# One core, long convolution beside routed experts: the first products, the transform of the input by pairs of positions, and two entries of the planner

## The chip, the cores and the metric

The kernel runs on one core of a Trainium2 chip. The core has a matrix engine (PE, whose weight loads are listed apart as PEld), a vector engine (DVE), a scalar engine (ACT), a general engine (POOL) and a queue engine (SP) that issues nearly all transfers. Its matmuls write to eight banks of accumulator memory. The metric is the device time of one execution in microseconds (us), lower is better. Before the change it is 1466.44 us, the median of 3 runs (1465.94 to 1466.64).

## The reference

2048 tokens `x` of width 576 pass through two branches that a gate mixes.

```python
g = sigmoid((x * gate_w).sum(-1))
# a: a long convolution of each of 576 channels with a generated filter of 2048 taps
K = einsum("dn,dnl,dn->dl", Cc, exp(dt * A * l), dt * Bc).real
a = irfft(rfft(x padded) * rfft(K padded))[:L] + x * Dskip
# b: 32 heads, two best of 64 keys on each of two sides, two best pairs, 4096 experts
s1, s2 = (x @ w_q)[..., :128] @ k1.T, (x @ w_q)[..., 128:] @ k2.T
top_s, top_e = two best of the sums of the two best of s1 and s2
b = sum over heads and choices of softmax(top_s) * gelu(x . u[top_e]) * v[top_e]
return g * a + (1 - g) * b
```

## The kernel before

All of it is written as generators in `body`, which a planner at build time interleaves. The planner keeps a clock (`clock`), a time at which each tile is ready (`rdy`, filled from costs in `act_cost`, `dve_cost`, `dma` L199 and `mm` L206), and counts of free banks (tags `sc`, `kb`, `wb`) and SBUF slots. What it makes is a fixed order of instructions for each engine. At run time nothing is reordered: an engine that meets an instruction whose input is late waits, and all behind it waits too.

**Split words.** The large products take float32 operands as two float16 words, a high and a low one. A group of 14 matmuls with 512 columns (`triple` L850) makes one bank: four slices of 128 of the contraction with three products each (high by high, high by low, low by high), and two matmuls for the last 64 rows, where high and low words are stacked (`wrem`, and slice 8 of `xb`). There are two families of 128 groups. Groups `s` are the key scores of 128 tokens and 8 heads (weights folded from `wq` and `kT` by `w_half` L518 and `wb` matmuls into `whl`). Groups `a` are the products of 128 experts of a block (`uhl`) with 512 tokens (`xb`), stored as `go` to `g_d`. Four token blocks `tb` and eight weight blocks `c` exist of each. After them follow, for each tile of 128 tokens, the one-hot products `S` and 192 matmuls `o`.

**The start.** SP loads `kT`, token block 0 (`xs`, `xr`), then the first score weights `wq`, then the first expert block (`us`, `ur`). `x_build` L446 squares the token block, bounds its norm by `x` matmuls with a matrix of ones, scales, and makes nine slices `xb`. `w_half` squares, folds and scales `wq`. `u_build` L1214 does the same for `us`. The main loop at L1563 picks `s` or `a` groups by readiness; the first one is an `s` group.

**The transform of the input** (`u_stage1` L977) takes 32 pairs of token positions, one a step, in two alternating generators `half(0)` and `half(1)`. A step loads 64 rows twice (so that the high words stand on partitions 0 to 63 and the low words on 64 to 127), loads a table `tu`, splits (`uh`: one ACT instruction and one DVE instruction on 64 partitions), runs 2 by 2 matmuls `u` of 128 rows and 288 columns, copies out and stores to `su_d`.

**The filter.** `k_front` L717 and `k_gen` make filter taps (phases by matmuls `kP`, taps by matmuls `kb`) in 36 chunks for `k_d`, on banks of tag `kb`, which the `u` matmuls share. When the last chunk is stored, `freq` L1164 loads the taps back in four parts (`ksb`) and then two tables `tk`, runs 32 steps `k` (`k_stage1` L1027), and then 36 steps of `products` L1063 (matmuls `pr`, `pi`, complex products on POOL and DVE, matmuls `pv`). The `s` and `a` groups fill PE between them.

## Time and profile before

| | us |
|---|---|
| median of 3 runs | 1466.44 |
| the profiled execution, its own time | 1466.58 |
| span of its trace, first to last instruction | 1464.7 |
| PE busy in the span | 1431.2 |
| DVE / ACT / POOL busy | 1248.5 / 790.6 / 532.0 |
| slots of `u` matmuls, first and last start | 114.8 to 558.6 |
| slots of `k` matmuls, first and last start | 662.9 to 739.0 |

The times in a trace count from the first instruction. Matmuls overlap in the records, since each is shown with its way through the array; how often they start tells what one costs in a stream. A timeline row names start, length, engine, line, operation, output and inputs, shape and count, and in brackets the idle time before it and what ended it.

### The profile page before, as it was taken

The numbers are of one execution on the slowest core, as the hardware profiler recorded it, in microseconds if no ns is written. First come the engines' busy times: TensorE is split into PE (matmuls) and PEld (weight loads), VectorE is DVE, ScalarE is ACT, GpSimd is POOL, SyncE is SP. The second block draws the span as 40 slices with busy tenths as digits, with TensorE's granted clock in tenths as the row PEclk, the third lists the DMA queues.
The fourth block names the chain that finished last, engine by engine and source line by source line (L and its number), as shares of the span: only waits on it lengthen the run. The fifth ranks groups of instructions, "written<-read, shape, count | busy, mean of one in ns | idle before, by whom it ended". The sixth has DMA issues, their size and how long they took to land.

```text
span 1464.7 us, 36789 instructions
## 1 busy us (share of the span) xinstructions
PE 1431.2 (98%) x14025; PEld 858.4 (59%) x14028; DVE 1248.5 (85%) x4589; ACT 790.6 (54%) x1315; POOL 532.0 (36%) x511
## 2 busy tenths in 40 slices
PE   5999999999999999999999999998999999999999
PEld 2445454554544544555555444455787787788787
DVE  6989989989999699959899898579998998898860
ACT  5647767698697787434656544576424224223310
POOL 0443545556745645201246799622100110110100
PEclk8999999999999999999999999999999999999999
DMA  9235433372434534384768666677533432442400
GB/s 319 81 93 162 128 94 118 111 213 89 147 104 133 160 107 135 109 263 138 254 211 290 232 200 206 221 239 221 157 111 116 133 125 85 138 147 68 156 10 17
DMA packets 139185, 221.21 MB, mean 151 GB/s; under 512 B 11648, under 2 KB 82688, under 8 KB 132608
## 3 DMA queue, kind: packets, MB, share of 16 engines
q1 hardware_dynamic: 138912, 218.78, 46.5%
q8 instruction: 110, 1.80, 0.5%
q14 instruction: 67, 0.55, 0.1%
q10 hardware_dynamic: 96, 0.07, 0.0%
HBM read 147.51 MB, written 71.30 MB: 149 GB/s over the span
## 4 chain that ended last, share of the span: by engine, by line
PE 84%; DVE 10%; DMA 3%; ACT 1%; issue 1%; SPq 1%; POOL 1%; DVEq 0%; ACTq 0%; POOLq 0%
PE o L213 24%; PE a L213 23%; PE s L213 22%; PE S L213 4%; PE wb L213 2%; PE kb L213 2%; DVE i L133 2%; PE pr L213 2%; DVE m L133 1%; PE u L213 1%; PE y L213 1%; PE kP L213 1%; DVE e L133 1%; PE pv L213 1%; DVE uh L133 1%
## 5 line engine op out<-in xcount | busy, mean ns | idle before, releaser
L213 PE MATMUL o<-vhl,wh 128*128 128x288 f16 x3072 | 387.0, 286 | 0.0
L213 PE MATMUL s<-whl,xb 128*128 128x512 f16 x1536 | 369.5, 382 | 5.0 <-DVE whl L133 4.2
L213 PE MATMUL a<-xb,uhl 128*128 128x512 f16 x1536 | 361.1, 379 | 0.4 <-DVE ko L133 0.4
L213 PEld LDWEIGHTS <-wh 128*128 128x128 f16 x3072 | 296.0, 98 | 76.3 <-issue 3.7
L213 PEld LDWEIGHTS <-xb 128*128 128x128 f16 x1792 | 171.8, 98 | 213.1 <-issue 27.1
L213 PEld LDWEIGHTS <-uhl 128*128 128x128 f16 x1536 | 148.2, 98 | 175.7 <-issue 2.8
L133 DVE FIND_INDEX8 i<-m,s 128x8 uint32<-128x64 f32 x1024 | 206.5, 222 | 0.0
L133 ACT ACTIVATE wh<-gl,s_wg 128x1024 f16<-128x1024 f32 x64 | 68.9, 1137 | 200.3 <-DVE gl L133 200.3
L133 DVE MAX8 m<-s 128x8 f32<-128x64 f32 x1024 | 146.4, 215 | 28.1 <-PE s L213 27.8
L133 POOL TENSOR_TENSOR CS<-CS,ex 128x512 f32<-128x512 f32 x72 | 100.2, 1423 | 139.0 <-DVE ex L133 120.0
L133 POOL TENSOR_TENSOR ya<-ya,db 128x576 f32<-128x576 f32 x16 | 32.0, 2012 | 305.2 <-DMA ya<-in_au_dram 143.6
L133 ACT ACTIVATE go<-a,i_a 128x512 f32<-128x512 f32 x95 | 64.2, 686 | 82.5 <-PE a L213 54.7
L133 POOL TENSOR_TENSOR e<-aN,rt 128x512 f32<-128x512 f32 x72 | 87.5, 1234 | 50.9 <-PE kb L213 47.6
L133 DVE SCALAR_TENSOR_TENSOR wh<-gl,s_wg,wh 128x1024 f16<-128x1024 f32 x64 | 92.4, 1474 | 11.3 <-ACT wh L133 11.3
L133 DVE TENSOR_TENSOR gl<-S,gl 128x256 f32<-128x256 f32 x256 | 90.0, 415 | 7.3 <-PE S L213 7.3
L133 DVE TENSOR_TENSOR Bg<-Be,vals 128x1024 f16<-128x1024 f16 x128 | 90.6, 749 | 2.2
L133 ACT ACTIVATE gl<-gl 128x1024 f32<-128x1024 f32 x64 | 63.5, 1045 | 34.8 <-DMA gl<-g_d 34.8
L133 DVE TENSOR_TENSOR A<-iota_a,vals 128x2048 f16<-128x2048 f16 x64 | 80.5, 1258 | 0.0
L213 PE MATMUL S<-Bg,A 128*128 128x64 f16 x2048 | 73.0, 193 | 5.1 <-DVE Bg L133 4.2
L213 PEld LDWEIGHTS <-A 128*128 128x128 f16 x2048 | 70.6, 97 | 11.2 <-DVE Bg L133 4.1
L213 PE MATMUL s<-wrem,xb 128*128 128x512 f16 x256 | 76.2, 379 | 0.0
L213 PE MATMUL a<-xb,wrem 128*128 128x512 f16 x256 | 76.2, 379 | 0.0
(203 smaller groups left out, 2205.7 us busy)
## 6 DMA issues: line engine op xcount, KB each, us to landing
g_d<-go SPq DMA_DIRECT2D x128, 256.0 KB, 2.7
gl<-g_d SPq DMA_DIRECT2D x32, 1024.0 KB, 5.4
wq<-in_wq_dram SPq DMA_DIRECT2D x16, 1152.0 KB, 6.3
us<-in_au_dram SPq DMA_DIRECT2D x64, 144.0 KB, 3.0
su_d<-us SPq DMA_DIRECT2D x32, 288.0 KB, 2.6
sk_d<-k1o SPq DMA_DIRECT2D x32, 288.0 KB, 2.8
vn<-in_vv_dram SPq DMA_DIRECT2D x32, 288.0 KB, 3.7
ui<-su_d SPq DMA_DIRECT2D x16, 576.0 KB, 4.0
```

Source lines behind the costliest of these rows:

```text
L133: return f(*a, **k)
L213: T.matmul(o, l, r, start=start, stop=stop)
```

## The change

- The first group of work is now the four `a` groups of token block 0 and expert block 0. SP loads `xr` and `xs` (in two halves), then `ur` and `us` (in two halves), then `kT`, token block 1, `wq` and the constants. A new `x_first` makes `xb` of block 0 from a bound on the sum of squares (`scale_first`: squares with accumulation, three narrow matmuls), as `u_build(0)` does. `x_norm` sends eight further `x` matmuls whose result is overwritten. The four groups are issued slice by slice across four banks, low words of `us` last.
- The folding of the first `wq` waits for token block 1, the rest of the tokens for the first slices.
- `u_stage1` takes two pairs of positions a step: one pair on partitions 0 to 63 and one on 64 to 127. High and low words stand beside each other in `uh` (128 partitions, two blocks of columns), and a step has 12 `u` matmuls of 64 rows each, alternating between the two halves of partitions. It asks for four banks at once. When it is behind the filter (`hungry`), new `kP` matmuls wait for it.
- The planner counts transfers of float16 and bfloat16 with two bytes an element, not four.
- The tables `tk` are loaded ahead of `ksb`.
- The main loop's end waits until the pools of the gating are closed (`shut`).

```diff
-    tu = np.ascontiguousarray(stacked(U_PAIRS).reshape(128, 32, 2, 128))
+    tu = stacked(U_PAIRS)[0].reshape(R2, 16, 2, 2, 128).transpose(2, 0, 1, 3, 4)
+    tu = np.ascontiguousarray(tu.reshape(128, 16, 2, 128))
...
-        wire[0] = max(wire[0], t) + 4 * o.shape[0] * size(o) / 3.4e5
+        wire[0] = max(wire[0], t) + (2 if o.dtype in (F16, BF16) else 4) * o.shape[0] * size(o) / 3.4e5
...
+    def halves_load(a, src, c):
+
+        columns.add(a.tensor.name)
+        for m in (0, 2):
+            dma(a[:, m:m + 2], src[128 * m:128 * m + 256, c].rearrange("(k p) n -> p k n", p=128))
...
-        dma(a, xT[0:512, c].rearrange("(k p) n -> p k n", p=128))
+        if tb > 0:
+            dma(a, xT[0:512, c].rearrange("(k p) n -> p k n", p=128))
         dma(r[0:64], xT[512:576, c])
         dma(r[64:128], xT[512:576, c])
+        if tb == 0:
+            halves_load(a, xT, c)
...
+    marks = {"x": [], "s": [], "h": [], "u": []}
+    first_u = [None, None]
+    ahead, normed = [], []
+
+    def x_norm(tb, sq):
+
+        yield from need("kb")
+        p = bank("kb", f"x{tb}")
+        if tb == 0:
+            for k in range(8):
+                mm(p, onesb, sq[:, k % 4, :], True, True)
+            while not marks["s"]:
+                yield 0.1
+        for k in range(5):
+            mm(p, onesb, sq[:, k, :], k == 0, k == 4)
+        normed.append(tb)
...
+    def x_first():
+
+        a, r = xl.pop(0)
+        b = slot([9, 512], F16, "xb0")
+        first_u[1] = b
+        ahead.append(slot([9, 512], F16, "xb1"))
+        sq = ahead[0][:, 0:5].bitcast(BF16)
+        s, i = yield from scale_first(a, r, sq)
+        spawn(x_norm(0, sq))
+        V.tensor_copy(i_x[:, 0:1], i)
+        for k in range(5):
+            while k == 2 and not marks["s"]:
+                yield 0.1
+            o, lo, src = (b[:, k], b[:, 4 + k], a[:, k, :]) if k < 4 else (b[:, 8], b[64:128, 8], r)
+            p = slice(0, 128) if k < 4 else slice(64, 128)
+            V.tensor_scalar(o, src, s, None, op0=OP.mult)
+            V.scalar_tensor_tensor(lo, src[p], s[p], o[p], op0=OP.mult, op1=OP.subtract)
+            marks["x"].append(V.free + 0.28)
...
+    def scale_first(a, r, sq, keep=None):
+
+        acc = [newcol() for _ in range(3)]
+        yield from ready(r)
+        S.activation(sq[:, 4], r, AF.Square, accum_out=sc[:, acc[0]])
+        for n, m in enumerate((0, 2)):
+            yield from ready(a[:, m:m + 2])
+            S.activation(sq[:, m:m + 2], a[:, m:m + 2], AF.Square, accum_out=sc[:, acc[n + 1]])
+        yield from ready(sq)
+        yield from need("kb")
+        p = bank("kb", "sq")
+        for n in range(3):
+            mm(p[:, 0:1], onesb, short(acc[n].start, 1), n == 0, n == 2, 0.05)
+        yield from ready(p)
+        out = root_scale(p[:, 0:1], 1.02)
...
-        while tb and 0 not in uhl:
+        while tb - 1 not in normed or len(marks["h"]) < 5 or tb > 1 and 0 not in whl:
             yield 0.3
-        b = slot([9, 512], F16, f"xb{tb}")
+        b = ahead.pop() if ahead else slot([9, 512], F16, f"xb{tb}")
...
+    folded = []
+
+    def fold_first(h, w, pbs):
+        while len(folded) < h or 1 not in scaled:
+            yield 0.2
+        out = []
+        yield from need("kb", 3 + h)
+        yield from w_fold(0, h, w, out, ("kb",) * 3)
+        pbs.extend(out)
+        folded.append(h)
...
+        if c == 0:
+            spawn(fold_first(h, w, pbs))
+        while 1 not in scaled:
+            yield 0.2
...
-            yield from w_fold(c, h, w, pbs, ("kb", "kb", "kb") if h == 0 else ("kb", "sc", "sc"))
...
+    hungry = [False]
...
+            while hungry[0]:
+                yield 0.2
             yield from need("kb")
             p = bank("kb", f"kP{c}_{z}")
...
-        def half(m):
-            for n in range(m, 2 * NT, 2):
-                a, o = us[:, m, :], us[:, 2 + m, :]
-                for z in range(2):
-                    l, far = U_PAIRS[n]
-                    dma(a[64 * z:64 * z + 64], bass.AP(tensor=au.tensor, offset=au.offset + l * D,
...
-                tu = uf.tile([128, 2, 128], F16, tag="tu", name=f"tu{n}", bufs=2)
-                dma(tu, tu_d[:, n])
-                yield from ready(a, tu)
-                h = uf.tile([128, D], F16, tag="uh", name=f"uh{n}", bufs=2)
-                S.activation(h, a, AF.Copy, scale=s_u)
-                yield from ready(h)
-                V.scalar_tensor_tensor(h[64:128], a[64:128], s_u[64:128], h[64:128], op0=OP.mult, op1=OP.subtract)
...
+        def load(p):
+            a = us[:, p % 2, :]
+            for g in range(2):
+                l, far = U_PAIRS[2 * p + g]
+                dma(a[64 * g:64 * g + 64], bass.AP(tensor=au.tensor, offset=au.offset + l * D,
+                                                   ap=[[64 * D, R1], [(far - l) * D, 2], [1, D]]))
+            tu = uf.tile([128, 2, 128], F16, tag="tu", name=f"tu{p}", bufs=2)
+            dma(tu, tu_d[:, p])
+            ld[p] = a, tu
...
-                    for z in range(2):
-                        mm(pb[:, :288], tu[:, z], h[:, 288 * hh:288 * hh + 288], z == 0, z == 1)
...
+        load(0)
+        for p in range(NT):
+            a, tu = ld.pop(p)
+            yield from ready(a, tu)
+            while ended[0] < p - 1:
+                yield 0.3
+            h = uf.tile([128, 2, D], F16, tag="uh", name=f"uh{p}", bufs=2)
+            S.activation(h[:, 0], a, AF.Copy, scale=s_u)
+            yield from ready(h)
+            V.scalar_tensor_tensor(h[:, 1], a, s_u, h[:, 0], op0=OP.mult, op1=OP.subtract)
+            if p + 1 < NT:
+                load(p + 1)
+            yield from ready(h)
+            while ended[0] < p:
+                yield 0.3
+            tag = side()
+            hungry[0] = p * NCK < 17 * kdone[0]
+            yield from need(tag, 4)
+            hungry[0] = False
+            pbs = [[bank(tag, f"u1_{p}_{g}_{hh}") for g in range(2)] for hh in range(2)]
+            for hh in range(2):
+                cs = slice(288 * hh, 288 * hh + 288)
+                for n, (z, w) in enumerate(((0, 0), (0, 1), (1, 0))):
+                    for g in range(2):
+                        r = slice(64 * g, 64 * g + 64)
+                        mm(pbs[hh][g][:, :288], tu[r, z], h[r, w, cs], n == 0, n == 2, 0.063)
+            spawn(tail(p, tag, pbs))
+            del pbs
+            yield 12
...
-        def load(w0):
-            tkt = fk.tile([128, 16, 2, 128], F16, tag="tk", name=f"tk{w0}", bufs=2)
-            dma(tkt, tk_d[:, w0:w0 + 16, :])
-            return tkt
-
-        tabs = load(0), load(16)
...
+        fk = FK.__enter__()
+        tabs = [fk.tile([128, 16, 2, 128], F16, tag="tk", name=f"tk{w0}", bufs=2) for w0 in (0, 16)]
+        for w0, tkt in zip((0, 16), tabs):
+            dma(tkt, tk_d[:, w0:w0 + 16, :])
         for j in range(4):
             while wire[0] > clock[0] + 2:
...
+        if c == 0:
+            first_u[0] = hl
+            s, i = yield from scale_first(a, r, sq, nu[:, 0:1])
+            marks["s"].append(1)
...
+        if c == 0:
+            for k in range(4):
+                S.activation(hl[:, 0, k, :], a[:, k, :], AF.Copy, scale=s)
+                marks["h"].append(S.free + 0.28)
+            S.activation(rem[:, 0, :], r, AF.Copy, scale=s)
+            marks["h"].append(S.free + 0.28)
         for k in range(4):
-            yield from split(hl[:, 0, k, :], hl[:, 1, k, :], a[:, k, :], s)
-        S.activation(rem[:, 0, :], r, AF.Copy, scale=s)
+            if c:
+                yield from split(hl[:, 0, k, :], hl[:, 1, k, :], a[:, k, :], s)
+                continue
+            while 0 not in scaled:
+                yield 0.1
+            rdy[key(hl)] = marks["h"][k]
+            V.scalar_tensor_tensor(hl[:, 1, k, :], a[:, k, :], s, hl[:, 0, k, :], op0=OP.mult, op1=OP.subtract)
+            marks["u"].append(V.free + 0.28)
...
+    xl = {0: x_load(0)}
+    take("raw", "raw")
+    xl["u"] = u_load(0)
     dma(kt, kT)
-    xl = {0: x_load(0)}
+    xl[1] = x_load(1)
     w_load(0, 0)
     w_load(0, 1)
+    dma(cst, cst_d[:, :KT])
...
-    spawn(k_split())
-    spawn(w_build(0))
-    spawn(w_half(0, 0, wl[0, 0]))
-    spawn(w_half(0, 1, wl[0, 1]))
-    for tb in range(4):
-        spawn(x_build(tb), 3 * tb)
-    spawn(u_build(0), 4)
+    spawn(x_first())
+    spawn(u_build(0))
+    spawn(w_build(0), 4)
+    spawn(w_half(0, 0, wl[0, 0]), 4)
+    spawn(w_half(0, 1, wl[0, 1]), 4)
+    spawn(k_split(), 4)
+    for tb in range(1, 4):
+        spawn(x_build(tb), 5 * tb)
...
+    until(lambda: marks["x"] and marks["h"], 0.1)
+    first = [bank("sc", f"a0_0_{j}") for j in range(4)]
+
+    def landed(kind, k):
+        until(lambda: len(marks[kind]) > k, 0.1)
+        idle(max(0.0, marks[kind][k] - clock[0]))
+
+    for w, n in ((0, 9), (1, 5)):
+        for xk in [x for k in range(4) for x in (k, 4 + k)[:2 - w]] + [8]:
+            k = 4 if xk == 8 else xk % 4
+            landed("x", k)
+            landed("hu"[w], k)
+            for j in range(4):
+                cs = slice(128 * j, 128 * j + 128)
+                mm(first[j], wrems[0][:, w, cs] if k == 4 else first_u[0][:, w, k, cs], first_u[1][:, xk, :],
+                   w == 0 and xk == 0, w == 1 and k == 4)
+            pump()
+    del acts[0:4]
+    if 0 in i_u:
+        V.tensor_scalar(i_a[:, 0, 0:1], i_x[:, 0:1], i_u[0], None, op0=OP.mult)
+    for j in range(4):
+        spawn(act_post(0, 0, j, first[j]))
...
-    until(lambda: min(stored) == 32 and ab)
+    until(lambda: min(stored) == 32 and shut)
```

The change moves instructions on every engine; three places follow. ACT's order from the start of the program, before (`xb` there is scratch for squares of tokens, `wj` for squares of score weights, `uhl` for squares of the expert block):

```order
L133 ACTIVATE vals<-kt 128x128
L133 ACTIVATE xb_136<-xs_119 128x1024
L133 ACTIVATE xb_136<-xr_120 128x512
L133 ACTIVATE wj_0_163,sc<-wq_0_124 128x1152 x2
L133 ACTIVATE wj_1_223,sc<-wq_1_126 128x1152 x2
L133 ACTIVATE whl_135<-wb_0_2_167,sci 128x2x256
L133 ACTIVATE wrem_116<-wb_0_4_168,sci 64x128 x4
L133 ACTIVATE uhl_282,sc<-us_142 128x2048
```

And in the change:

```order
L134 ACTIVATE xb_149,sc<-xr_119 128x512
L134 ACTIVATE xb_149,sc<-xs_118 128x1024 x2
L134 ACTIVATE uhl_150,sc<-ur_125 128x512
L134 ACTIVATE uhl_150,sc<-us_124 128x1024 x2
L134 ACTIVATE uhl_150<-us_124,sci 128x512 x4
L134 ACTIVATE wrem_114<-ur_125,sci 128x512
L134 ACTIVATE vals<-kt 128x128
L134 ACTIVATE xb_149<-xs_131 128x2048
L134 ACTIVATE xb_149<-xr_132 128x512
```

All work on the expert block moves ahead of the keys, token block 1 and the score weights.

PE's order at the first step of the input's transform, before (`tu` is the table, `uh` the split input, `s_15` a score group that goes on around it):

```order
L213 MATMUL s_15_1214<-whl_135,xb_736 128x512
L213 LDWEIGHTS tu_1119
L213 MATMUL u_0_0_1250<-uh_1168,tu_1119 128x288
L213 LDWEIGHTS tu_1119
L213 MATMUL u_0_0_1250<-uh_1168,tu_1119 128x288
L213 LDWEIGHTS xb_736
```

And in the change, from the fifth to the eighth of the 12 matmuls of a step:

```order
L214 MATMUL u_0_0_0_1079<-uh_963,tu_916 128x288
L214 LDWEIGHTS tu_916
L214 MATMUL u_0_1_0_1080<-uh_963,tu_916 128x288
L214 LDWEIGHTS tu_916
L214 MATMUL u_0_0_1_1081<-uh_963,tu_916 128x288
L214 LDWEIGHTS tu_916
L214 MATMUL u_0_1_1_1082<-uh_963,tu_916 128x288
```

Pieces of two matmuls become one piece of twelve, in which the banks of the first and the second pair of positions (`u_0_0_0` and `u_0_1_0`, then `u_0_0_1` and `u_0_1_1`) alternate.

SP's order after the last chunk of the filter, before (`k_d` holds the taps, `ksb` takes them back, `tk` are the tables, `wq` score weights):

```order
L204 DMA k_d<-ko 128x1024
L204 DMA ksb<-k_d 128x18x256
L204 DMA wq_1_7753<-in_wq_dram 128x2304
L204 DMA g_d<-go_1_0_7783 128x4x128
L204 DMA ksb<-k_d 128x18x256
L204 DMA g_d<-go_1_1_7804 128x4x128
L204 DMA g_d<-go_1_2_7823 128x4x128
L204 DMA g_d<-go_1_3_7844 128x4x128
L204 DMA ksb<-k_d 128x18x256
L204 DMA wq_0_7905<-in_wq_dram 128x2304
L204 DMA g_d<-go_2_0_7925 128x4x128
L204 DMA g_d<-go_2_1_7937 128x4x128
```

And in the change:

```order
L205 DMA k_d<-ko 128x1024
L205 DMA wq_0_8151<-in_wq_dram 128x2304
L205 DMA tk_8166<-in_tk_dram 128x4096
L205 DMA tk_8167<-in_tk_dram 128x4096
L205 DMA ksb<-k_d 128x18x256
L205 DMA g_d<-go_0_1_8288 128x4x128
L205 DMA ksb<-k_d 128x18x256
L205 DMA wq_1_8341<-in_wq_dram 128x2304
L205 DMA g_d<-go_0_2_8352 128x4x128
L205 DMA g_d<-go_0_3_8378 128x4x128
L205 DMA ksb<-k_d 128x18x256
L205 DMA g_d<-go_1_0_8398 128x4x128
```

The tables stand ahead of the taps, and fewer other transfers stand between the four parts of the taps. Between the last `kb` matmuls and the first `k` matmul PE has about 17 groups of 14 in the order before and 12 in the order of the change; between the last `kb` and the last `pv` it has 76.6 and 67.

118 lines of the change are left out of this document (65 added, 53 removed).

## The prediction

> **What bounds the kernel now.** First the page's head and the table by stages, to see which engine sets the time, and where it doesn't.
>
> ```profile
> span 1464.7 us, 36789 instructions
> PE 1431.2 (98%) x14025; PEld 858.4 (59%) x14028; DVE 1248.5 (85%) x4589; ACT 790.6 (54%) x1315; POOL 532.0 (36%) x511
> ```
>
> ```profile
> 0.00:26.34 26.34, 9.21 (x157) 6.66 (x158) 17.13 (x52) 18.39 (x33) 0.20 (x4) 0.88 0.94 333
> 26.34:605.00 578.66, 575.68 (x5149) 287.05 (x5155) 521.85 (x1990) 416.34 (x611) 305.08 (x238) 1.00 0.41 125
> 605.00:742.00 137.00, 135.04 (x1142) 73.00 (x1133) 110.72 (x793) 67.36 (x176) 17.53 (x58) 1.00 0.65 215
> 742.00:940.00 198.00, 196.33 (x1854) 94.69 (x1851) 170.23 (x1076) 103.73 (x278) 157.88 (x182) 0.99 0.65 220
> 940.00:1050.00 110.00, 104.34 (x1061) 65.04 (x1063) 96.53 (x155) 66.16 (x100) 26.73 (x18) 1.00 0.69 215
> 1050.00:1461.20 411.20, 410.61 (x4694) 331.95 (x4686) 331.58 (x528) 118.64 (x120) 24.61 (x12) 1.00 0.33 105
> ```
>
> The second column of a stage is its length, the third PE's busy time. PE is idle for 1461.20 - 1431.22 = 30.0 us, and 26.34 - 9.21 = 17.1 us of that lie before 26.34. The stages after it lose 3.0, 2.0, 1.7, 5.7 and 0.6, together 12.9. So all work outside PE is covered, and a change gains only by fewer PE slots, or by an earlier start, or out of those 12.9. Then the timeline of the start, with the sizes of its loads.
>
> ```profile
> 6.84 1.06 ACT L133 ACTIVATE xb<-xs 128x1024 bf16<-128x1024 f32 x1 [3.75 <-DMA xs<-in_xT_dram]
> 7.95 2.29 PE L213 MATMUL x<-xb,onesb 128*128 128x512 bf16 x5 [4.54 <-ACT xb L133]
> 10.79 1.16 ACT L133 ACTIVATE wj<-wq 128x1152 bf16<-128x1152 f32 x1 [2.37 <-DMA wq<-in_wq_dram]
> 11.71 1.67 DVE L133 TENSOR_SCALAR xb<-xs,sci 128x512 f16<-128x512 f32 x4
> 11.86 0.19 ACT L133 ACTIVATION_READ_ACCUMULATOR wj<-wq 128x1 f32 x1
> 14.21 0.20 PE L213 MATMUL wn<-sc,onesb 128*128 128x1 bf16 x2
> 14.35 2.32 PE L213 MATMUL wb<-kt,wq 128*64 128x64 f32 x72
> 14.90 0.22 DVE L133 TENSOR_SCALAR sci<-sci 128x1 int32<-128x1 int32 x2
> 15.23 0.74 DVE L133 SCALAR_TENSOR_TENSOR xb<-xs,sci,xb 128x512 f16<-128x512 f32 x1
> 23.47 2.56 ACT L133 ACTIVATE uhl<-us,sci 128x512 f16<-128x512 f32 x4
> 25.94 0.71 ACT L133 ACTIVATE wrem<-ur,sci 128x512 f16<-128x512 f32 x1
> 26.34 4.50 PE L213 MATMUL s<-whl,xb 128*128 128x512 f16 x11 [4.20 <-DVE whl L133]
> 31.10 2.75 PE L213 MATMUL s<-whl,xb 128*128 128x512 f16 x12
> ```
>
> ```profile
> wq<-in_wq_dram SPq DMA_DIRECT2D x16, 1152.0 KB, 6.3
> xs<-in_xT_dram SPq DMA_DIRECT2D x4, 1024.0 KB, 6.4
> xr<-in_xT_dram SPq DMA_DIRECT2D x8, 128.0 KB, 5.8
> ```
>
> PE's steady work begins at 26.34, after waits of 4.54 (the five `x` matmuls) and 4.20 us (the 11 `s`) among others. What it waits for last is a chain: load `wq`, square, fold, scale, split `whl`. The first 11 matmuls are slow: (4.50 - 0.38) / 10 = 0.41 us from start to start, against (2.75 - 0.38) / 11 = 0.216 later (0.38 is one matmul's own way). That loses some 1.9 us more.
>
> **The start, step by step.** In the new order 1024 + 256 KB of tokens and as much of the expert block come first, 2560 KB (`us` and `ur` have the sizes of `xs` and `xr`). Before, ACT began on the first `wq` at 10.79, when 64 + 1024 + 256 + 1152 = 2496 KB stood at or ahead of it in the queue. So the second half of `us` is there at about 11.0. ACT's squares of a half take 1.06 and reading the sum 0.19: 12.25. Narrow matmuls and scale took 14.90 + 0.22 - 14.21 = 0.91: 13.2. A slice of `uhl` takes 2.56 / 4 = 0.64: 13.8, and with a hop PE starts at 14.0.
>
> Does it then run through? A slice's step is four matmuls, 0.86 us, and there are two steps a slice, so PE wants a new `uhl` slice every 1.73; ACT delivers one every 0.64 and the last by 13.2 + 2.56 + 0.71 = 16.5. DVE makes a slice of `xb` in 1.67 / 4 + 0.74 = 1.16; two are made between the tokens' scale (their loads end near 7, scale near 9.3) and the experts' scale, the other three by 13.4 + 3 x 1.16 = 16.9, the last wanted at 14.0 + 8 x 0.86 = 20.9. The five low words of `us` follow, 5 x 0.74: 20.6, and the first of them is wanted at 14.0 + 9 x 0.86 = 21.7. Token block 1 is squared behind `uhl` (2 x 1.06 and half of that again for `xr`), so its norm, scale and ten slices end near 27; PE comes to it at 14.0 + 56 x 0.216 + 1.1 + 2.32 = 29.5, past the norm and the first fold. So ACT and DVE are hidden, with 2 to 4 us to spare. The eight extra `x` matmuls stand in time in which PE has nothing: from some 8.4, at 0.46 each (2.29 us for five), to 12.1.
>
> What had PE done by 26.34 that it must still do after 14.0? Two folds, 2 x 2.32, the `wn`, 2 x 0.20, and one `s`, 0.22: 5.3. The lead is (26.34 + 1.9) - (14.0 + 5.3) = 8.9 us. Bounds: loads 1 us earlier give 10. Loads 1 us later, first matmuls as slow as at 26.34 (1.9) and 1 us of waits between slices give 5. I take 8.9, as each step has its row.
>
> **The input's transform.** Its rows, then how closely matmuls follow each other there and at three changes of shape.
>
> ```profile
> L213 PE MATMUL u<-uh,tu x128: 283/286/297, 114.8 to 558.6; 128*128 128x288 f16 x128
> L133 ACT ACTIVATE uh<-us,sci x32: 758/764/820, 109.4 to 547.0; 128x576 f16<-128x576 f32 x32
> L133 DVE SCALAR_TENSOR_TENSOR uh<-us,sci,uh x32: 818/1488/1931, 112.9 to 553.8; 64x576 f16<-64x576 f32 x32
> ...
> L213 PEld LDWEIGHTS <-tu x128: 95/98/99, 114.7 to 558.4; 128*128 128x128 f16 x128
> ```
>
> ```profile
> 154.64 1.03 PE L213 MATMUL s<-whl,xb 128*128 128x512 f16 x4
> 155.60 0.32 PE L213 MATMUL kb<-Y,CS 128*32 128x64 f32 x8
> ...
> 163.38 0.41 PE L213 MATMUL u<-uh,tu 128*128 128x288 f16 x2
> 163.63 1.67 PE L213 MATMUL a<-xb,uhl 128*128 128x512 f16 x7
> ...
> 756.37 0.33 PE L213 MATMUL pr<-ui,cst 64*64 64x192 f32 x2
> ...
> 756.53 0.22 PE L213 MATMUL pr<-ki,cst 64*64 64x64 f32 x2
> ```
>
> ```profile
> L213 PE MATMUL S<-Bg,A 128*128 128x64 f16 x2048 | 73.0, 193 | 5.1 <-DVE Bg L133 4.2
> ```
>
> A `u` matmul costs (163.63 - 163.38) / 2 = 0.125 of PE's stream; 128 of them 16.0 us. Now there are 192 on half the rows, in 96 couples. That halves run side by side shows in `pr`: four matmuls on the four quarters of the array, two of them above and two below, pass in 0.16 (756.53 - 756.37). So 96 x 0.13 = 12.5. Each step of twelve changes the array's shape twice. Between four `s` and the first `kb` lie 0.96 us where 4 x 0.216 = 0.86 are due: 0.1 a change, 16 x 2 x 0.1 = 3.2. Sum 15.7, a gain of 0.3: nothing. Bounds: no change cost gives -3.5; halves in sequence 192 x 0.125 + 3.2 - 16.0 = +11.2.
>
> Each couple has two weight loads, each 97 ns long by the `tu` row. If loads queued up, a couple would take 0.194, not 0.13. But 2048 `S` matmuls, each with its own load, pass in 73.0 us, 36 ns apart, so loads overlap; two in 0.13 fit. I take the row of `S`. The Trainium skill (TensorE: Matmul & The Clock Gate, LDWEIGHTS) says that a load's time goes by its columns and not its rows, 128 / 1.2 = 107 ns here. By that, if loads don't overlap, the estimate would be 96 x 0.213 + 3.2 - 16.0 = +7.7 us. The length agrees with the trace's 95 to 99 ns; the spacing of `S` speaks against the sum.
>
> ACT loses 16 splits of 0.77 (12.3 us) and DVE 16 of 1.4, if 128 partitions take as long as 64 (22.4); 48 of 96 loads go. PE had waited for these only 0.7 us, so I take nothing; the cover is the fill of `s` and `a`. `need(tag, 4)` takes all banks of the filter, and behind it wait `kP` and `kb`. In the order the last `kb` comes after 172 fill groups, not 161.
>
> **The filter's way back.** That is what becomes tighter: from the last `kb` to the last `pv` PE has 67 fill groups, not 76.6, so 9.6 x 14 x 0.216 = 29 us less cover.
>
> ```profile
> L213 PE MATMUL k<-ksb,tk x128: 283/286/296, 662.9 to 739.0; 128*128 128x288 f16 x128
> ...
> L204 SPq DMA_DIRECT2D tk<-in_tk_dram x2: 424/2638/4852, 640.9 to 645.8; - x2
> ...
> DMA to landing us min/median/max: 8.6/9.8/11.0
> ```
>
> ```profile
> L133 DVE TENSOR_TENSOR ko<-kb,ko x18: 670/681/693, 160.2 to 609.3; 128x512 f16<-128x512 f32 x18
> ```
>
> ```profile
> 640.00:650.00 10.00, 10.00 (x48) 4.58 (x47) 7.54 (x66) 2.51 (x4) 0.00 (x0) 1.00 0.99 315
> ```
>
> Before, the last table landed by 645.8 + 8.6 = 654.4 and `k` began at 662.9: 8.5 us that nobody waited for. Now SP must move, past the last `k_d`, two `wq`, two tables of 1024 KB, four parts of 128 x 18 x 256 x 2 B = 1152 KB and three `g_d` of 256 KB: 10.0 MB, at the 315 GB/s of a full stretch 31.6 us. With store and landing (3.3 + 2.3) that is 37 us after the last `kb`; PE comes after 12 groups and two folds, 36.3 + 4.6 = 41 us. So moving the tables and counting two bytes cost nothing, 4 us to spare. `products`: POOL is busy 157.9 of 198 us before; 3.5 of the 9.6 groups go there, so 187 us must hold the same work. It fits at 84%, with a fixed order made from planned costs. I add 1.5 us to the waits of 605 to 940 and take 1.5 off the 5.7 us at 940 to 1050, where 10.8 fill groups stand after the first `S` instead of 9.6. Bounds: 0 and +29; -4. The wait for `shut` moves nothing that the trace shows late.
>
> **Sum**, against the profiled 1466.6 (span 1464.7 and 1.9 around it; the median is 0.1 lower): 1466.6 - 8.9 - 0.3 + 1.5 - 1.5 = 1457.4, so 1457 for the median.
>
> **Rivals.** (1) *The filter's way back takes as long as before, and PE waits for it*: a fixed order can't fill the hole. It decides once the chain from the last `kb` to the last `pv` needs more than 330 - 29 = 301 us. For it: POOL's 84% and `k` steps that waited 2.0 us already; against it: 8.5 us unused ahead of `k`. Full price 1457 + 29 = 1486; from 9 us on the kernel is slower than before. 0.12 for over 6 us. (2) *Weight loads or halves in sequence*: 96 x 0.194 + 3.2 - 16.0 = +5.8, 1463; halves +11.2, 1468, no change. Against both, `S` and `pr`. 0.05. (3) *Half a start*: late loads, slow first matmuls and waits between slices, lead 4 to 5, 1461 to 1462. For it: 26.34's slow matmuls. 0.11. (4) *More*: DVE's and ACT's 35 freed us close half of the 12.9 elsewhere: 1457 - 6.4 = 1451. Against it: PE's waits there were mostly behind one-hots and stores. 0.12. The forecast, 1452 to 1461, has 0.60.
>
> **How the numbers follow.** A difference under about 0.2% (2.9 us) can't be told from none. Faster: 0.60 + 0.11 + 0.12 = 0.83. Of (1) 0.07 is slower and 0.05 the same; (2) counts as the same: 0.10 and 0.07. The range 1450 to 1465 leaves out most of (1), (2) with its halves in sequence and a rest of (4).
>
> **What would show it.** Right: first `a` matmul at 13 to 15, 0.216 apart from the first; PE idle before 100 us near 13; `u` couples 0.13 apart, twelve in 0.8; `k` begins without a wait on `ksb`; idle from 605 to 940 under 7. Wrong: an `a` matmul waiting on `xb` or `uhl` again and again; `pr` waiting on POOL or DVE; a hole ahead of the first `k`.

## The result, and the profile after

The changed kernel takes 1455.86 us (median of 6 runs, 1453.85 to 1459.65) where the kernel before, run beside it, takes 1466.54 (1465.36 to 1467.70). The ratio is 0.9927, with a 95% interval of 0.9917 to 0.9937: 10.7 us faster. The prediction's time was 1457. The profiled execution is one of the longer ones, 1458.63 us. Of the runs behind the experiments below, one (of the kernel with the start alone) took 2489 us at a granted clock of 0.558, and is left out of that kernel's figures.

The page's head, and the table by stages, cut where the start now ends. Its columns are the stage, its length, the busy time of PE, PEld, DVE, ACT and POOL, the granted clock, the DMA share and GB/s.

```profile
span 1456.8 us, 36814 instructions
PE 1430.8 (98%) x14103; PEld 853.9 (59%) x14105; DVE 1221.0 (84%) x4569; ACT 776.0 (53%) x1304; POOL 521.4 (36%) x510
```

```profile
0.00:14.60 14.60, 5.51 (x19) 2.19 (x19) 5.27 (x22) 8.19 (x16) 0.20 (x4) 1.00 0.86 276
14.60:605.00 590.40, 585.47 (x5372) 290.10 (x5374) 516.05 (x2214) 402.95 (x603) 282.72 (x228) 1.00 0.37 116
605.00:742.00 137.00, 137.00 (x1192) 72.95 (x1190) 107.70 (x701) 73.52 (x171) 24.50 (x49) 1.00 0.66 215
742.00:940.00 198.00, 196.06 (x1929) 96.43 (x1928) 168.47 (x976) 109.88 (x310) 163.23 (x200) 1.00 0.71 242
940.00:1050.00 110.00, 104.04 (x1008) 66.44 (x1006) 103.11 (x147) 69.99 (x95) 26.89 (x17) 0.97 0.70 224
1050.00:1453.20 403.20, 402.71 (x4595) 325.80 (x4591) 319.88 (x514) 111.46 (x112) 23.85 (x12) 1.00 0.32 102
```

PE's busy time is what it was (1430.8 for 1431.2), though DVE has 27 and ACT 15 us less to do. Idle before the steady work begins: 14.60 - 5.51 = 9.1 us, where it was 17.1. The later stages lose 4.9, 0.0, 1.9, 6.0 and 0.5, together 13.3; before they lost 12.9. Between these two profiles, then, the gain lies in the start and nowhere else. Its timeline:

```profile
9.44 3.57 PE L214 MATMUL x<-xb,onesb 128*128 128x512 bf16 x8
11.80 1.06 ACT L134 ACTIVATE uhl<-us 128x1024 bf16<-128x1024 f32 x1 [0.23 <-DMA us<-in_uT_dram]
13.02 1.65 PE L214 MATMUL x<-xb,onesb 128*128 128x512 bf16 x5
13.83 2.56 ACT L134 ACTIVATE uhl<-us,sci 128x512 f16<-128x512 f32 x4 [0.88 <-DVE sci L134]
14.61 2.76 PE L214 MATMUL a<-xb,uhl 128*128 128x512 f16 x12
```

The first `a` is at 14.61, and twelve pass in 2.76 us: (2.76 - 0.38) / 11 = 0.216 from start to start, full rate at once. PE's steady stream starts 26.34 - 14.61 = 11.7 us earlier; behind that point it is busy for 1430.8 - 5.5 = 1425.3 us, before for 1431.2 - 9.2 = 1422.0. The lead is 11.7 - 3.3 = 8.4 us.

The largest of the later losses stands in the change from the last fill groups to `S` and `o`. The timeline of three engines around this hole, and two stretches of the windows behind it (`Bg` are the one-hots that `S` multiplies, `ya` is the part of `y` that comes from the input itself, `vhl` the split words of `v`):

```profile
1007.72 3.50 DVE L134 TENSOR_TENSOR Bg<-Be,vals 128x1024 f16<-128x1024 f16 x2
...
1008.82 3.67 POOL L134 TENSOR_TENSOR ya<-ya,db 128x576 f32<-128x576 f32 x2
...
1018.37 4.25 POOL L134 TENSOR_TENSOR ya<-ya,db 128x576 f32<-128x576 f32 x2 [5.88 <-DMA ya<-in_au_dram]
...
1019.39 3.85 DVE L134 SCALAR_TENSOR_TENSOR vhl<-vs,sci,vhl 128x576 f16<-128x576 f32 x2
...
1027.19 1.29 DVE L134 TENSOR_TENSOR Bg<-Be,vals 128x1024 f16<-128x1024 f16 x2
...
1027.94 0.23 PE L214 MATMUL S<-Bg,A 128*128 128x64 f16 x1 [4.57 <-DVE Bg L134]
```

```profile
1027.64:1034.47 6.83, 6.17 (x51) 4.39 (x52) 6.79 (x15) 0.00 (x0) 0.00 (x0) 0.50 0.30 128
1034.47:1041.30 6.83, 6.83 (x87) 5.38 (x89) 5.22 (x11) 3.49 (x4) 0.00 (x0) 1.00 0.19 47
```

PE waits 4.57 us for one-hots (`Bg`) that DVE makes late. Two `Bg` take 3.50 us on DVE while POOL works, and 1.29 us at 1027.19, when it doesn't. From the end of the hole on, the granted clock is 0.50 for 6.83 us; 51 PE instructions pass there, and 87 in the same time afterwards. So the hole costs its own 4.6 us and, by these counts, 2 to 3 more. The runs of 1453.85 to 1456.02 us have a mean clock of 0.999 or 1.000, the profiled one 0.998, the longest 0.996. So the shortest has next to no half clock; that its hole is smaller too is likely, but it has no trace.

### The profile page after: what moved, and what is told of

The parts are those of the page before. It is cut to its first block, busy times and chain, and to the rows that moved or that the text cites. A ratio compares the mean times of both kernels' runs of the same rounds, so it can differ in the third digit from the quotient of the medians.

```text
span 1456.8 us, 36814 instructions
## 1 busy us (share of the span) xinstructions
PE 1430.8 (98%) x14103; PEld 853.9 (59%) x14105; DVE 1221.0 (84%) x4569; ACT 776.0 (53%) x1304; POOL 521.4 (36%) x510
## 4 chain that ended last, share of the span: by engine, by line
PE 85%; DVE 5%; DMA 2%; ACT 1%; issue 0%; POOL 0%; SPq 0%; DVEq 0%; POOLq 0%
PE o L214 25%; PE s L214 22%; PE a L214 22%; PE S L214 4%; PE kb L214 2%; PE wb L214 2%; PE pr L214 2%; DMA vn<-in_au_dram 1%; PE y L214 1%; PE kP L214 1%; PE k L214 1%; DVE i L134 1%; PE pv L214 1%; PE u L214 1%; DVE vhl L134 1%; DVE m L134 1%
## 5 line engine op out<-in xcount | busy, mean ns | idle before, releaser
L214 PE MATMUL s<-whl,xb 128*128 128x512 f16 x1536 | 365.0, 379 | 0.0
L134 POOL TENSOR_TENSOR e<-aN,rt 128x512 f32<-128x512 f32 x72 | 83.1, 1174 | 49.9 <-PE kb L214 43.8
L134 DVE MATCH_VALUE_LOAD i<-m,s 128x8 f32 x1024 | 76.3, 75 | 0.1
```

Of the source, the lines that this page charges most:

```text
L134: return f(*a, **k)
L214: T.matmul(o, l, r, start=start, stop=stop)
```

## The experiments

Two profiles whose idle time differs in little but the start suggest that the rest of the change does nothing. Twelve kernels were run to see whether that is so: first the change in three parts (the **start**; the **pairs**, two token positions a step in `u`; the **planner**, which is two bytes for half words, tap tables ahead of taps, and the condition `shut`), each alone and by twos.

This table has all of them. Idle is PE's, in us, by windows (0 to 42, 42 to 605, 605 to 940, 940 to 1100 us); "half" is the time after 42 us at a granted clock of 0.50; "kb-pv" is the time from the start of the last `kb` to that of the last `pv`, and the last column that `pv`'s place in the written order, in fill groups (14 `s` and `a` matmuls each, 256 in all).

```
kernel              median  ratio to before [95%]      idle by window        half  kb-pv  pv at
before              1466.5                           17.2  2.9  3.6  5.7     3.4   329.9  237.6
whole change        1455.9  0.9927 [.9917, .9937]     9.3  4.8  1.9  6.4     6.8   293.5  238.9
e1 start            1462.8  0.9975 [.9965, .9986]     9.7  9.7  3.4  4.7     3.4   318.7  233.6
e2 pairs+planner    1473.0  1.0038 [1.0024, 1.0051]  16.8  1.1  4.4  9.8     6.8   306.6  237.2
e3 pairs            1484.3  1.0121 [1.0106, 1.0137]  16.9  1.8  5.9 17.2    13.7   309.2  240.2
e4 planner          1470.8  1.0030 [1.0020, 1.0041]  17.3  4.1  7.0  2.3    10.2   290.1  228.2
e5 start+pairs      1484.7  1.0120 [1.0104, 1.0136]  10.4  4.6  3.1 24.6    20.5   312.0  242.6
e6 start+planner    1467.3  1.0000 [.9990, 1.0010]    9.2  3.7  5.6  6.9     6.8   283.5  235.6
e7 no extra x       1460.0  0.9945 [.9926, .9964]    13.7  5.0  1.9  5.3    10.2   293.3  238.9
e8 ya on DVE        1452.6  0.9902 [.9886, .9918]    10.5  4.4  2.8  0.3     0.0   294.3  238.9
e9 tables late      1472.5  1.0035 [1.0021, 1.0048]   9.8  4.7  2.5 13.9    17.1   306.1  242.0
e10 four bytes      1503.9  1.0242 [1.0228, 1.0256]   9.5  4.5  2.9 40.4    47.8   340.6  252.6
e11 halves apart    1453.2  0.9900 [.9885, .9915]    10.3  4.7  2.8  2.9     0.0   294.4  238.9
e12 e2, ya on DVE   1473.5  1.0036 [1.0022, 1.0050]  17.0  1.1  4.5 10.3     3.4   306.7  237.2
```

The medians are those of all runs of a kernel; the columns behind the ratio come from its one profiled execution, whose own time lies up to 3.5 us off the median (e7 3.5 above, e1 3.0 above, the whole change 2.8 above, e6 2.6 below). The kernel before, run again beside each group, took 1466.5, 1466.5, 1466.8 and 1467.4 us. So differences of 1 to 3 us between kernels of this table are not to be read closely.

**e1: the start alone.** The kernel before with the new loads, squares and first groups, and nothing else:

```diff
+    def halves_load(a, src, c):
...
+        for m in (0, 2):
+            dma(a[:, m:m + 2], src[128 * m:128 * m + 256, c].rearrange("(k p) n -> p k n", p=128))
```

> Contains the new start alone (activations loaded first, the square and the scale ahead of the first products, first groups at full rate with the extra x matmuls in the dead time); the u step, the planner's bytes and the place of the tap tables are those of before. Theory (the start is all of the gain): PE's stream starts about 12 us earlier, with some 3.7 us of work no longer done ahead of it, so about 8.4 us are gained: 1457 to 1460 us, 6.5 to 9.5 us under before; idle time of PE before 15 us near 9, elsewhere 10 to 16. Rival A (the pairs, by the time that they free on DVE and ACT, carry half or more): at most 4 us under before. Rival B (any edit moves the written order, and the order is worth a few us either way): idle time of PE outside the start off 13 by over 4 us.

1462.8, 3.7 us under before, not 6.5 to 9.5. The start does what it should: idle up to 42 us falls by 7.5. But 42 to 605 us lose 9.7 us where before had 2.9, in eleven waits of 0.3 to 1.8 us for `uhl`, `uh`, `CS`, `ko`, `whl` and `i`. Rival A's bound (at most 4) is met, and rival B's too (17.8 us of idle time in the windows behind the start, where before had 12.2).

**e2, e3, e4: the rest, and its parts.** In e3 the core of the edit to `u` is

```diff
-                    for z in range(2):
-                        mm(pb[:, :288], tu[:, z], h[:, 288 * hh:288 * hh + 288], z == 0, z == 1)
+                for n, (z, w) in enumerate(((0, 0), (0, 1), (1, 0))):
+                    for g in range(2):
+                        r = slice(64 * g, 64 * g + 64)
+                        mm(pbs[hh][g][:, :288], tu[r, z], h[r, w, cs], n == 0, n == 2, 0.063)
```

and in e4 the planner's

```diff
-        wire[0] = max(wire[0], t) + 4 * o.shape[0] * size(o) / 3.4e5
+        wire[0] = max(wire[0], t) + (2 if o.dtype in (F16, BF16) else 4) * o.shape[0] * size(o) / 3.4e5
```

with the tables' two loads ahead of the taps'. e2 has both.

> Contains everything but the new start: two token positions a step in u, two bytes for half words in the planner, tap tables ahead of taps, the earlier-closing condition. Theory: within 3 us of before (1463.5 to 1469.5), idle time of PE before 27 us still 17. Rival A: 4 us or more under before, with less idle time of PE at 605 to 1050 us. Rival B: off before by over 4 us with idle time of PE outside the start changed by as much.

> Contains the two token positions a step in u alone. Theory: 12 us less on ACT and 22 us less on DVE end no wait of PE, and 192 half-height matmuls, two by two, cost what 128 full ones cost: within 3 us of before. Rival A: 5 us or more under before. Rival C (the filter's way back, which now begins later in fill groups, ends late and is waited for at 605 to 740 us): 5 us or more above before, with the idle time of PE there over 7 us.

> Contains the planner's two bytes for half words, the tap tables ahead of the taps and the condition on which the last loop ends, nothing else. Theory: within 3 us of before, since no wait of PE there is one for a table or a planned transfer. Rival D (the planner's transfers, now counted right, move work into the holes at 605 to 1050 us): 4 us or more under before, idle time of PE there at most 5 us where it was 9.4.

All three are slower than before: by 6.5, 17.8 and 4.3 us. The theory (within 3 us each) falls three times, and rivals A and D, which had e2, e3 and e4 faster, fall too. Rival B is met in e2 by the time and not by the idle time behind the start, which rose by 3.1 us. Rival C had the sign of e3 and the wrong place: PE loses 1.1 us at 605 to 740 us, and 17.2 at 940 to 1100, where before lost 5.7. PE's waits in e3, in us, times and longest:

```profile
PE S L214 <- DVE Bg L134: 13.3, 9, 6.3
...
PE o L214 <- POOL vhl L134: 3.8, 1, 3.8
```

**e5, e6: the start with one part.**

> Start and pairs of the change, the planner's bytes, the place of the tap tables and the closing condition as before. Theory now (the start alone lost in the first 605 us what it had won, since PE then begins 12 us earlier on a DVE that has as much to do; the pairs take 22 us off DVE): idle time of PE between the first a and 605 us back to 3 to 6 us from the 9.9 of the start alone; the time 1455 to 1462 unless the change of S and o at 940 to 1100 us is late as with the pairs alone (13.3 + 3.8 us idle there), then 1464 to 1470. Rival B (the written order is a lottery at every stage): idle time of 8 us or more before 605 us all the same.

> Start and planner of the change, u as before with one half of a token position's rows a step. Theory: DVE has 22 us more to do than in the whole change, so 8 us or more idle between the first a and 605 us, 1461 to 1466. Rival D (the planner's bytes are what makes the start pay): 5 us or less idle there, 1454 to 1459.

e5 takes 1484.7: the start's whole gain (idle up to 42 us 10.4 for 16.9) is lost again at 940 to 1100 us. Its window there and the waits:

```profile
940.00:1100.00 160.00, 135.44 (x1436) 92.25 (x1435) 135.53 (x207) 85.46 (x127) 37.65 (x26) 0.94 0.59 191
```

```profile
PE S L214 <- DVE Bg L134: 16.7, 7, 7.6
...
PE o L214 <- POOL vhl L134: 3.8, 2, 2.6
```

e5 brings the idle time of 42 to 605 us from 9.7 to 4.6, as the theory said, but its time lies far above the 1464 to 1470 that had been set for a late change to `S`. e6 was to lose 8 us or more at 42 to 605 with a fuller DVE, and loses 3.7. The window in e1, then in e6:

```profile
42.00:605.00 563.00, 553.26 (x5150) 277.73 (x5150) 512.00 (x1901) 396.52 (x582) 293.66 (x234) 1.00 0.41 124
```

```profile
42.00:605.00 563.00, 559.33 (x4952) 279.33 (x4953) 494.38 (x2032) 396.63 (x590) 280.49 (x223) 1.00 0.41 123
```

DVE is busy for 494.4 us there in e6, as in e5 (494.3) and not as in e1 (512.0): the planner also put other work into this stretch. Before has 509.6 and loses only 2.9. So e6 doesn't test DVE's load by itself, and whether the load or the order cost e1 those microseconds stays open. Rival D fails as well: its idle time is there, its 1454 to 1459 us are not. e6 equals before.

Before takes 1466.5; the parts give 1462.8 (start), 1484.3 (pairs), 1470.8 (planner), 1484.7, 1467.3, 1473.0 and 1455.9 together. The start is worth 3.7 us alone, 3.5 with the planner, nothing with the pairs, and 17.1 with both. The single effects sum to -3.7 + 17.8 + 4.3 = +18.4, the whole is -10.7.

**e9, e10: what of the planner the pairs need.** The whole change with the tap tables behind the taps (e9), and with four bytes for half words (e10):

```diff
-        fk = FK.__enter__()
-        tabs = [fk.tile([128, 16, 2, 128], F16, tag="tk", name=f"tk{w0}", bufs=2) for w0 in (0, 16)]
...
+        tabs = load(0), load(16)
```

```diff
-        wire[0] = max(wire[0], t) + (2 if o.dtype in (F16, BF16) else 4) * o.shape[0] * size(o) / 3.4e5
+        wire[0] = max(wire[0], t) + 4 * o.shape[0] * size(o) / 3.4e5
```

> The whole change with the tap tables loaded after the taps, as before. The order has k's first products at fill group 181.9 where the whole change has 184.0, v's last at 242.0 for 238.9 and S's first at 247.0 for 245.2. Theory now (what decides between these kernels is how late v's last product comes against S's first, since v's last steps and S's first share DVE and POOL): some 4 to 6 us more idle at 940 to 1100 us, 1459 to 1466. Rival E (the tap tables in front are what the pairs need): 1475 or more.

> The whole change with four bytes counted for half words, as before. The order has k from group 191.6 and v's last at 252.6, S's first at 256.0, behind all fill groups. Theory now: DVE and POOL finish v while S waits, with no fill groups left: 20 us or more idle at 940 to 1100 us and half clock behind the holes, 1480 to 1495. Rival F (the bytes only shift the plan, the chip's holes are elsewhere): within 5 us of the whole change.

Both go the way of the theory and farther than its figures: 16.6 and 48.1 us above the whole change's median, for 3 to 10 and 24 to 39; e9 lies nearer to rival E's 1475 than to 1466, and rival F (within 5 us) falls. Up to 605 us the traces agree with that of the whole change (4.7 and 4.5 us of idle time, 4.8). Then in e10 the planner takes the taps' 1152 KB for twice as long, and puts `k` and all that follows behind more fill groups. Rows by form of e9, then of e10, the last number ahead of the semicolon being the start of the last one:

```profile
L214 PE MATMUL k<-ksb,tk x128: 283/286/286, 670.3 to 749.6; 128*128 128x288 f16 x128
...
L214 PE MATMUL pv<-vf,cst x288: 376/376/427, 773.3 to 943.7; 64*64 64x256 f32 x144
```

```profile
L214 PE MATMUL k<-ksb,tk x128: 282/286/286, 704.9 to 800.0; 128*128 128x288 f16 x128
...
L214 PE MATMUL pv<-vf,cst x288: 376/376/427, 822.4 to 978.3; 64*64 64x256 f32 x144
...
L214 PE MATMUL S<-Bg,A x2048: 190/193/257, 988.7 to 1445.5; 128*128 128x64 f16 x187
```

The same rows of the whole change, with its last `kb`:

```profile
L214 PE MATMUL kb<-e,CS x1152: 219/219/243, 164.5 to 637.0; 128*32 128x64 f32 x192
...
L214 PE MATMUL k<-ksb,tk x128: 282/286/286, 678.7 to 744.2; 128*128 128x288 f16 x128
...
L214 PE MATMUL pv<-vf,cst x288: 376/376/427, 771.3 to 930.5; 64*64 64x256 f32 x144
...
L214 PE MATMUL S<-Bg,A x2048: 190/193/241, 954.8 to 1400.0; 128*128 128x64 f16 x187
```

There the last `pv` begins 24 us ahead of the first `S`; in e10 it is 10 us. The windows of e10 and e9 from 940 us on, and e10's waits:

```profile
940.00:1100.00 160.00, 119.57 (x1292) 76.97 (x1290) 134.14 (x205) 77.79 (x114) 64.11 (x53) 0.85 0.62 206
```

```profile
940.00:1100.00 160.00, 146.06 (x1596) 101.31 (x1595) 143.61 (x227) 84.27 (x122) 36.02 (x26) 0.96 0.59 191
```

```profile
PE S L214 <- DVE Bg L134: 27.8, 12, 8.8
...
PE y L214 <- DMA tf<-in_tf_dram: 8.8, 1, 8.8
```

POOL is busy for 64.1 us in e10's window: the end of `products` has slid into the time in which DVE must make one-hots, and by its order the first `S` stands behind all 256 fill groups, so that PE has none left to run beside them. Which of the two counts more, the late work or the missing fill, these runs don't separate.

The two entries also need each other. Against e5, which has neither (1484.7), the bytes alone (e9) win 12.3 us, the tables in front alone (e10) lose 19.2, and both together win 28.9.

**e7: without the eight extra `x` matmuls.** They compute nothing that is used; the planner counts them as before, so that only PE's list is shorter.

```diff
-                mm(p, onesb, sq[:, k % 4, :], True, True)
+                mm(p, onesb, sq[:, k % 4, :], True, True, plan=True)
```

> The whole change with the eight extra x matmuls not issued (they compute nothing that is used). Theory: PE then stands idle for some 4 us before the first a, which begins at half rate, 0.41 to 0.43 us apart for some 7 to 10 us: 1.5 to 4 us above the whole change, PE's first granted clock at 0.5. Rival: no loss (within 0.5 us), since the clock holds over such a gap or the time comes back later.

```profile
14.35 2.30 PE L215 MATMUL x<-xb,onesb 128*128 128x512 bf16 x5
16.43 4.50 PE L215 MATMUL a<-xb,uhl 128*128 128x512 f16 x12
```

Twelve `a` take 4.50 us, not 2.76, and the five `x` 2.30, not 1.65: 2.4 us lost at the lower rate. The median is 4.1 us above the whole change, of which the trace shows these 2.4; the runs of the two overlap (1456.13 to 1464.24 and 1453.85 to 1459.65), so the size isn't settled. In this profiled run the loads also came in 1.3 us later, which is no part of the edit. The theory holds for the rate of the first `a`, (4.50 - 0.38) / 11 = 0.37 us apart in the mean, and not for its 7 to 10 us: the next twelve, from 20.82 on, take 2.75. The clock's first record in this profile comes only at 20 us.

**e8: `ya` on DVE.** The two multiplies of the first part of `y`, which stood on POOL at 1008.82:

```diff
-                G.tensor_mul(a, a, db)
+                (G if p else V).tensor_mul(a, a, db)
```

> The whole change with the two multiplies of y's first part that stood on POOL moved to DVE, in their place in the order. Theory (POOL's multiplies stretch the DVE work beside them at 1008 and 1018 us): the DVE operations there take 0.7 to 1.3 us each again, the hole of PE at 1023 us shrinks from 4.6 to under 2.5 us and the half clock behind it goes: 2 to 6 us under the whole change. Rival (DVE is simply full there): the hole stays at 4 us or grows by the 1.2 to 1.6 us that the multiplies take on DVE.

```profile
1015.16 1.41 DVE L134 TENSOR_TENSOR ya<-ya,db 128x576 f32<-128x576 f32 x2
...
1017.70 1.53 DVE L134 SCALAR_TENSOR_TENSOR vhl<-vs,sci,vhl 128x576 f16<-128x576 f32 x2
...
1019.24 2.80 POOL L134 TENSOR_TENSOR ya<-ya,db 128x576 f32<-128x576 f32 x2 [10.20 <-DVE vhl L134]
```

```profile
940.00:1100.00 160.00, 159.74 (x1732) 113.00 (x1733) 152.40 (x236) 88.89 (x116) 26.46 (x17) 1.00 0.63 203
```

PE idles for 0.3 us in that window instead of 6.4, and no half clock is left. The moved multiplies take 1.41 us on DVE, where they took 3.67 on POOL. The second pair still runs on POOL, but now behind the two `vhl` operations and not beside them: these take 1.53 us, which took 3.85. The theory holds. The median is 1452.6, 3.3 us under the whole change; its four runs (1450.44 to 1453.83) lie just below the six of the whole change (1453.85 to 1459.65), which were not run beside them. e11, which adds one edit that changes nothing, has the same ratio to before (0.9900). The planner also moved `S` matmuls behind some `o` from there on, so the gain is that of the edit with the order that follows from it, and not of the shorter operations alone.

**e11: halves in sequence.** On top of e8, the three products of one half of the rows, then three of the other; only PE's order of these 192 differs:

```diff
-                for n, (z, w) in enumerate(((0, 0), (0, 1), (1, 0))):
-                    for g in range(2):
+                for g in range(2):
+                    for n, (z, w) in enumerate(((0, 0), (0, 1), (1, 0))):
```

> The kernel with the two multiplies of y on DVE, and in u the three products of one half of the rows, then the three of the other, where the change alternates the halves; only PE's order of these 192 products differs. Theory: alternating is what lets two half-height products share the time of one, so the twelve of a step take some 0.3 to 0.7 us more each, 5 to 11 us over 16 steps, if halves in sequence do not overlap. Rival: the same time within 1 us, since PE takes the next product of either half as it comes.

```profile
205.06 0.92 PE L214 MATMUL u<-uh,tu 64*128 64x288 f16 x12
205.91 0.82 PE L214 MATMUL s<-whl,xb 128*128 128x512 f16 x3
```

Twelve take 205.91 - 205.06 = 0.85 us; in the whole change a step took 0.84 (below). The theory falls, the rival holds in the time: alternating is not what makes two half-height products share a time. Why the order doesn't matter isn't seen in the trace. The median, 1453.2, is that of e8 within the runs' spread.

**e12: e2 with `ya` on DVE.** The edit of e8 on the change without its start.

> All of the change but its start, with the two multiplies of y's first part on DVE. Theory (the start alone is worth some 9 us once the change to S has no hole in either kernel): 1460 to 1463 us, idle time at 940 to 1050 us under 3 us. Rival (the start is worth 17 us, as between the two kernels without this edit, and the rest is a loss by itself): 1467 or more.

1473.5, the same as e2: its 10.3 us of idle time at 940 to 1100 us (9.8 in e2) are other holes, among them waits of `S` of 3.3 and 1.5 us near 970 and of 2.2 at 1041, and one of `y` for `tf` of 1.0. The theory falls, the rival holds: the start is worth 17 us or more here too (20.9 against e8), and the whole change isn't the start plus a neutral rest.

## Why the prediction was right, and where it was not

**What bounds the kernel, and the start: right.** First `a` at 14.6 (14.0 forecast), full rate at once, and no `a` that waits for `xb` or `uhl`. The lead is 8.4 us where 8.9 stood in the sum. Counted by work it comes out nearly the same: by 80 us PE has begun 264 `s` and `a` matmuls where before had begun 226, and 38 x 0.216 = 8.2. Idle up to 42 us falls by 6.5 to 8.1 us in every kernel that has the new start with its extra `x`, against the same kernel without it. Rival 3 (half a start, 4 to 5) is out; e7 shows that the eight extra matmuls carry part of it, since without them the first matmuls run slower, 0.37 us apart for 0.216.

**The transform: the matmuls right, a wait missed.** A step of the whole change:

```profile
202.93 1.46 PE L214 MATMUL s<-whl,xb 128*128 128x512 f16 x6
204.32 0.91 PE L214 MATMUL u<-uh,tu 64*128 64x288 f16 x12
205.16 1.04 PE L214 MATMUL s<-whl,xb 128*128 128x512 f16 x4
```

From the first `u` to the next `s` lie 205.16 - 204.32 = 0.84 us, with one change of shape in it; the other stands ahead of the step, where six `s` take 204.32 - 202.93 = 1.39 us and 6 x 0.216 = 1.30 are due. So a step costs 0.93 us and sixteen 14.9, where 15.7 was forecast. But two early steps wait for `uh`, which the forecast had at nothing:

```profile
PE u L214 <- DVE uh L134: 1.9, 2, 1.4
```

With this the transform costs 16.8 us and not 15.7. Before it cost 16.0 and 0.7 of such waits, so it neither gains nor loses, where a gain of 0.3 was forecast. Rival 2 is out. A couple passes in (0.84 - 0.10) / 6 = 0.123 us, so its two loads of 97 ns each don't queue up, and e11 shows that this doesn't hang on the halves' order. By the Trainium skill (TensorE: Matmul & The Clock Gate, LDWEIGHTS) a load of 128 columns is estimated at 107 ns, which would be 0.213 a couple if two were added; the trace speaks against adding them.

**ACT's and DVE's freed time: nothing, as forecast.** Idle time behind the start is 13.3 us for 12.9, so rival 4, which had half of it closed, is out. The pairs alone free as much and are 17.8 us slower.

**"Moving the tables and counting two bytes cost nothing": this step failed, though it did not show in the time.** The filter's way back was worked out with the tables in front and came to 37 us against PE's 41; `k` in fact began without a wait on `ksb`, and 605 to 742 us have no idle time. What was missed is that this part carries the pairs. Taken away, it costs some 17 us (the tables' place), 48 (the bytes) or 29 (all of it, e5). Rival 1 (0.12) had the mechanism, and its point of decision: with the pairs, more than 301 us from the last `kb` to the last `pv`. The four kernels with the pairs and 293 to 294 us lose 0.3 to 6.4 us at 940 to 1100; the six with 306 to 341 us lose 9.8 to 40.4, and are all slower than before. Its full price of 1486 is near e3 and e5 (1484 and 1485), by luck, since the place was wrong: PE hardly waits at `k` or `products`, it waits where `S` begins, presumably because the planner lays the order out around a late chain. The forecast priced the cure at nothing because it never priced the kernel without it.

**"+1.5 and -1.5" at 605 to 940 and at 940 to 1050: both of the wrong sign, and small in this pair.** 605 to 940 lost 1.9 us where before lost 3.6; 940 to 1050 lost 6.0 where before lost 5.7. The stage ahead of 605, left at no change, lost 1.9 more. In the other kernels 940 to 1100 has 0.3 to 40 us of idle time. It was the place with the largest stake, and it had been costed by counting fill groups behind the first `S`, without asking how late the work ahead of `S` ends.

So the time was right because the start's 8.4 us are real, and because the rest of the whole change happens to leave as much idle time behind the start as before had; e1, e5 and e6, which have the start with less of the rest, have 4 to 20 us more. That part is luck, since the forecast had no reason for it that held. The last 2 to 3 us are not explained: the profiled run is 8.0 us under the profiled run of before, the sum had 9.2, and the median is 10.7 under, by runs without a trace. The sum's terms are no prices of the parts.

What is shown and what isn't: e9 and e10 each make one edit to the whole change, and with the chain grow the holes at 940 to 1100, from 6.4 to 13.9 and 40.4. That the chain's length decides in the other kernels is an order among them, no proof: the four short ones share their order up to there (but for `x` in e7 and `u` in e11), and for the kernels without the pairs the length says nothing (283 to 330 us, 2.3 to 6.9 us of holes). Why e2's holes are 9.8 us, with its last `pv` at group 237.2, ahead of the whole change's 238.9, is open.

## What to carry to other kernels

Where one planner writes the whole order, an edit's price is not a term in a sum: run the parts alone and together before any is called neutral or useless. When a middle stage is stretched, follow its last product to the next change of phase and ask there which engine makes the new phase's operands, and what else it still has to do. A hole of over 3.2 us in PE's stream cost more than its length here, since half a clock followed, so the largest hole behind a change of phase is the first to go after.

## What the hardware showed that had not been expected

- The clock after short holes. Behind every hole of over 3.2 us after the start a granted clock of 0.50 follows, for 3.4, 6.8 or up to 20.5 us, always a multiple of 3.41. Shorter holes go both ways: 1.67 us at 887 in the kernel before was followed by 3.41 us of it, 1.87 us in e11 and 3.03 in e5 were not. The Trainium skill (TensorE: Matmul & The Clock Gate, Part 1) has a window of about 3.4 us and says the clock falls after an idle window or more; the multiples agree, but more than half of the stretches of half clock here follow a hole shorter than a window.
- POOL beside DVE. In the whole change two `ya` multiplies on POOL and two `vhl` operations on DVE ran at once, from 1018.37 to 1019.39 + 3.85 = 1023.24: 4.87 us. In e8 the same two and two, one after another, take 2.80 and 1.53, together 4.33. Nothing was won by running them side by side. The Trainium skill (SBUF — State Buffer, "SBUF: two separate sides") says that a DVE operation with two inputs in SBUF and a POOL operation that reads SBUF lock a shared pair of ports against each other for a whole instruction, which agrees.
- Two half-height products of 288 columns pass in 0.123 us, about what one full one took before (0.125). With the halves in sequence a step of twelve takes 0.85 us instead of 0.84.
